# Hash-masked attention with a PReLU MLP: bits and turned q and k in one round, the last stores on ScalarE's queue, fewer products of zeros

## The chip, the cores and the metric

The kernel runs on one core of a Trainium2 chip. The metric is the device time of a whole execution in microseconds; the median of several executions is compared. A core has TensorE (PE in the profile, with PEld for its weight loads), VectorE (DVE), ScalarE (ACT), GpSimd (POOL) and SyncE (SP), which here issues most of the DMAs.

## The reference

The inputs are q, k and v of shape (4, 8, 768, 64), a projection of (64, 6), MLP weights of (512, 2048) and (2048, 512), and 2048 slopes alpha, all float32. Cut to what matters:

```python
q_bits = (einsum('bhsd,dk->bhsk', q, proj) > 0)        # the same for k
q_bucket = sum(q_bits * 2 ** arange(6))                # the same for k
mask = q_bucket[..., :, None] == k_bucket[..., None, :]
scores = where(mask, q @ k.T / sqrt(64), -1e9)
attn = exp(scores - max(scores)); attn = attn / (sum(attn) + 1e-9)
x = (attn @ v) -> (4 * 768, 512)
h = x @ w_in
out = (max(h, 0) + alpha * min(h, 0)) @ w_out
```

Each query sees only the keys whose six projected signs are the same as its own.

## The kernel before

`fast_path` does everything; a `general_path` follows that is skipped unless a flag, worked out from the sizes of the inputs, asks for it.

**Attention.** Two heads of one batch are a pair; there are 16 pairs, `pi` from 0 to 15. A pair's 768 queries are done in two halves of 384. One half of one pair is a unit, or round, `u = 2 * pi + g`, with `g` 0 or 1: 32 rounds. All instructions that go through `do(...)` keep their written order on their engine, so the loop over `u` is the order by hand; the DMA issues are placed around it. For one round the work is:

- `scores`: for each of six chunks of 128 keys, TensorE multiplies the signs of the hash bits (`qb`, `kb`, bf16) and then the turned k and q (`kT`, `qT`, f32) into one of three double banks of PSUM (tag `sc`); ScalarE writes the exponential to a tile `pt` (L706). Different bits push a score so far down that the exponential is zero. The second half of the keys of round `u` and the first half of round `u + 1` are done in one go.
- `add_first`, `add_last`, `add_total`: VectorE (L715, L720, L721, L724) and one accumulating DMA on GpSimd's queue (L716) add the six chunks to `accd`.
- `attend` and `totals`: TensorE multiplies v with the probabilities (`av`, L734) and ones with `accd` (`sm`, L746). `av` and `sm` have one buffer each.
- `divide`: VectorE takes the reciprocals of the totals, multiplies (L762) and the result `x` is stored to DRAM. The next round's `av` needs this to be done.
- `weight_abs`, `weight_parts`, `weight_sum`, `weight_sums`: one piece of the MLP weights per round is rounded and combined on ScalarE and VectorE, and stored to DRAM as the operands of a Strassen-like scheme of seven products.

Each pair needs three preparations. `turn(pi, name)` transposes q or k on TensorE (L649) and copies the result from PSUM to `qT` or `kT` (L654 on ScalarE, L652 on VectorE); these tiles have two buffers. `hash_bits(pi)` multiplies them with the projection on TensorE (L674) and writes the signs as `qb` and `kb`, seven activations on ScalarE (L682, L687). `magnitude(pi, name)` squares q or k in place on ScalarE (L660) and keeps the sums for the flag; after it the tile is free, and q or k of a later pair is loaded into it (three buffers, `qn` and `kn`). Before, rounds with `g == 0` do `hash_bits(pi + 1)`, and rounds with `g == 1` do `turn(pi + 2)` and `magnitude(pi)`, and then load pair `pi + 3`.

**The start.** `setup` fills constants and issues eight matmuls of zeros (`nil`, L512) while q and k of pair 0 are loaded in two halves, q on SyncE's queue and k on ScalarE's. Then both first halves are turned, the bits of the first half are made, and both second halves are turned. The first three chunks of scores follow.

**MLP.** From round 31 on, 8 blocks of the first layer (`f_0` to `f_7`) and 7 of the second (`z_1`, `z_2`, `z_5`, `z_6`, `z_3`, `z_7`, `z_4`) per batch run on TensorE, each itself split into seven products. A block's last step (`before.step(4)`) comes after the first step of the next. Result blocks that are complete wait in a list `to_turn`. `turn_out` transposes them on VectorE in 32 x 32 pieces (L946) and issues twelve stores of 32 KB on SyncE (L952). Only the last block, `z_4`, goes through `turn_last`: TensorE transposes it (L965), ScalarE copies it (L967), and SyncE stores it in two DMAs (L969). The tiles `o` that both use have two buffers.

Of the kernel before, what the change touches and what calls it, by code (L numbers as in the profile page):

```python
# [8 lines left out]
F32 = mybir.dt.float32  # L9
BF16 = mybir.dt.bfloat16  # L10
U32 = mybir.dt.uint32
AF = mybir.ActivationFunctionType
ALU = mybir.AluOpType
# [393 lines left out]
def fast_path(  # L407
# [12 lines left out]
    nc = tc.nc  # L420
# [37 lines left out]
    ones = const.tile([P, D], F32, name="ones")  # L458
    wh = const.tile([P, 32], F32, name="wh")
    hb = const.tile([P, 1], F32, name="hb")  # L460
    alpha16 = const.tile([NF, P], F32, name="alpha16")
    alpha = const.tile([P, NF], F32, name="alpha")
    mags = const.tile([P, 2, NPAIR], F32, name="mags")
# [27 lines left out]
    def load_part(pi, name, cs, queue):  # L491
# [4 lines left out]
        for s in range(2):  # L496
            queue.dma_start(nat[name, pi][:, cs, s], src[b, 2 * hp + s].rearrange("(p c) d -> p c d", c=NC)[:, cs])

    def setup():

        zero = const.tile([P, 512], BF16, name="zero")
        do(DVE.memset(zero, 0.0))
        do(DVE.memset(wh, 0.0))
        for s in range(2):
            nc.sync.dma_start(wh[D * s : D * s + D, :NB], proj)
        nc.sync.dma_start(alpha16, moe_alpha.rearrange("(t p) -> t p", p=P))
        make_identity(nc, ident)
        do(DVE.memset(ones, 1.0))

        ps = psum.tile([P, 512], F32, name="nil", tag="av")  # L510
        for i in range(8):
            do(PE.matmul(ps, zero[:, :P], zero, start=True, stop=True))  # L512

        do(DVE.memset(hb, 0.0))
        for r in range(0, P, 32):
            do(DVE.memset(hb[r : r + 2 * NB], 1.0 if r % D else -1.0))
            do(DVE.memset(hb[r : r + NB], -1e-37))
        for t in pts:
            do(POOL.memset(t[:, :, CW : CW + 1], 1.0))
        for t in qbs:  # L520
            do(POOL.memset(t, 0.0))
# [115 lines left out]
    def two_banks(name):  # L637
        return psum.tile([P, 2, 512], F32, name=name, tag="sc", bufs=3)
# [3 lines left out]
    def turn(pi, name, halves=BOTH, engine=None):  # L642

        src = nat[name, pi].rearrange("p c h d -> p c (h d)")
        if halves.start == 0:
            tr[name, pi] = pool.tile([P, S], F32, name=f"{name}T{pi}", tag=f"{name}T")
        ps = two_banks(f"tp_{name}{pi}")
        for c in range(CH * halves.start, CH * halves.stop):
            do(PE.transpose(ps[:, c // CH, c % CH * P :][:, :P], src[:, c], ident))  # L649
        dst = tr[name, pi].rearrange("p (h w) -> p h w", h=2)[:, halves]  # L650
        if engine is DVE:
            do(DVE.tensor_copy(dst, ps[:, halves, :CW]))  # L652
        else:
            do(ACT.activation(dst, ps[:, halves, :CW], AF.Copy, scale=DOWN if name == "q" else 1.0))  # L654
# [4 lines left out]
        n = "qk".index(name)  # L659
        do(ACT.activation(t, t, AF.Square, accum_out=mags[:, n, pi : pi + 1]))  # L660

    def hash_bits(pi, halves=BOTH):

        if halves.start == 0:
            bits["q", pi] = qbs[pi % 2]
            bits["k", pi] = pool.tile([P, S], BF16, name=f"kb{pi}", tag="kb")
        ps = two_banks(f"hs{pi}")
        for half in range(halves.start, halves.stop):  # L670
            for n, name in enumerate("kq"):
                for s in range(2):
                    r, c = D * s, D * (s ^ half) + 32 * n
                    do(PE.matmul(  # L674
                        ps[c : c + 32, half, :CW], wh[r : r + D], tr[name, pi][r : r + D, half * CW : (half + 1) * CW],
                        start=True, stop=True,
                    ))
        for half in range(halves.start, halves.stop):
            cols = slice(half * CW, (half + 1) * CW)
            for s in range(2):  # L680
                c = D * (s ^ half) + 32
                do(ACT.activation(  # L682
                    bits["q", pi][D * s : D * s + 32, cols], ps[c : c + 32, half, :CW], AF.Sign, bias=hb[c : c + 32],
                ))

            for to, c, n in [(0, 0, P)] if half == 0 else [(0, D, D), (D, 0, D)]:
                do(ACT.activation(  # L687
                    bits["k", pi][to : to + n, cols], ps[c : c + n, half, :CW], AF.Sign, bias=hb[c : c + n],
                ))


    def scores(u, half):
# [261 lines left out]
                        src[32 * a : 32 * a + 32, c],  # L954
                    )

    def turn_last():

        ((b, p, half, ch),) = to_turn
        ps = two_banks("to").rearrange("p a f -> p (a f)").rearrange("p (t i f) -> p t i f", i=2, f=P)  # L960
        o = late[0].tile([P, CH, P, 2], F32, name="o_last", tag="o")
        for ts in ((2,), (0, 1)):
            for i in range(2):
                for t in ts:
                    do(PE.transpose(ps[:, t, i], m2[b, p][:, i, t * P : (t + 1) * P], ident))  # L965
            ts = slice(ts[0], ts[-1] + 1)
            do(ACT.copy(o[:, ts].rearrange("p t f i -> p t i f"), ps[:, ts]))  # L967
            dst = out_v[b, ch * CH : (ch + 1) * CH].rearrange("c p d -> p c d")
            nc.sync.dma_start(dst[:, ts, half * 2 * P : (half + 1) * 2 * P], o[:, ts].rearrange("p t f i -> p t (f i)"))  # L969


    top = const.tile([P, 4], F32, name="top")
# [32 lines left out]
    for half in (first, second):  # L1005
        turn(0, "q", half)
        turn(0, "k", half, DVE)
        if half is first:
            hash_bits(0, first)
    load(1, "q")  # L1010
    load(1, "k")
    load_weight(0)
# [16 lines left out]
    for u in range(UNITS):  # L1029
        pi, g = divmod(u, NCH)  # L1030
        scores(u, 1)
        if u < last:
            scores(u + 1, 0)
        add_last(u)
        add_total(u)
        if u < last:
            add_first(u + 1)
        else:
            now = ff1(0, 0)
            now.step(1)  # L1040
            now.step(5)
        if g == 0 and pi + 1 < NPAIR:
            hash_bits(pi + 1)
        if g == 1 and pi + 2 < NPAIR:
            turn(pi + 2, "q")
            turn(pi + 2, "k")
        if u < last:
            weight_parts(u + 1)
        else:
            weight_sums(4)  # L1050
        attend(u, range(NC - 1))
        totals(u)
        if u < last:
            weight_sum(u + 1)
            weight_sums(1 if u < HW - 1 else 2)
            weight_group(u + 1)
        attend(u, range(NC - 1, NC))
        divide(u)
        if g == 1 and pi + 2 < NPAIR:
            load(pi + 2, "v")  # L1060
        load_weight(u + 4)
        if u == HW + 2:
            load_w(0)
            load_w(1)
            load_x(0)
        if HW + 4 <= u < HW + 8:
            sum_x(0, u - HW - 4, DVE)
        if u + 2 < NW:
            weight_abs(u + 2)
        if u == 1:  # L1070
            setup_alpha()
        if g == 1:
            for name in "qk":
                magnitude(pi, name)
                if pi + 3 < NPAIR:
                    load(pi + 3, name)


    late = []
# [5 lines left out]
    for j, (b, what, n) in enumerate(blocks):  # L1085
        n2 = n + 1 if what == "2" else 0 if n == NI - 1 else 7
        if n2 == 0:
            sides_g(b, 0)
            sum_w2(b, 0, 3, 4)
        now.step(2) if j else now.step(6)  # L1090
        if j == 0:
            now.step(3)
            now.step(7)
            now.step(2)
        now.step(22)
        if j == 4:
            largest()
        if 0 < n2 < 7:
            sides_g(b, n2)
            sum_w2(b, n2, 3, 4)  # L1100
        if n2 < 7:
            sum_g2(b, n2, 3, 4)
        if j:
            now.step(5)
            now.step(6)
            now.step(3)
            sum_w2(b, n2, 6)
            now.step(7)
            sum_w2(b, n2, 5)
            sum_g2(b, n2, 5)  # L1110
        if j == 4:
            verdict()
        if what == "1":
            load_w(b * NI + n + 2)
            if n >= NI - 2:
                load_w2(b, n - NI + 2)
        else:
            load_w2(b, n + 2)
            if b + 1 < B:
                if n == 0:  # L1120
                    load_x(b + 1)
                if n == 6:
                    for m in range(4):
                        sum_x(b + 1, m, DVE)
        turn_out()
        before = now
        if j + 1 < len(blocks):
            b1, what1, n1 = blocks[j + 1]
            now = ff1(b1, n1) if what1 == "1" else ff2(b1, n1)
            now.step(1)  # L1130
        before.step(4)
        if n2 < 7:
            sum_g2(b, n2, 6)
    turn_last()
# [1 line left out]
_INS = ['q', 'k', 'v', 'proj', 'moe_w_in', 'moe_w_out', 'moe_alpha']  # L1136
_OUTS = [((3072, 512), 'float32')]
# [25 lines left out]
```

## Time and profile before

| what | value |
|---|---|
| time, median of 4 runs | 922.04 us (920.7 to 923.46) |
| profiled execution, its own time | 923.68 us |
| its span, first to last instruction | 921.9 us |
| TensorE busy | 900.3 us (98%) |
| VectorE busy | 768.7 us (83%) |
| ScalarE busy | 409.9 us (44%) |
| GpSimd busy | 40.9 us (4%) |
| HBM traffic | 139 GB/s over the span |

The span is that of one profiled execution and runs from its first to its last instruction; the 1.8 us between span and time lie around it. All durations below come from this one execution. In rows of the timeline the first two numbers are the start and the duration in us, then come the engine, the line, the operation, its output and inputs with their shapes, and how many instructions the row holds; a bracket holds the idle time before it and what ended it. In rows by stage the columns are the stage and its length, busy time and instructions of PE, PEld, DVE, ACT and POOL, the granted clock of TensorE, the DMA share and GB/s. PEld overlaps PE. Matmuls are pipelined and their ends are modelled, so PE busy is not PE at its peak.

### The profile page before, as it was taken

The page shows a single profiled execution, that of the slowest core. Times are in us where ns is not written, and L with a number is a line of the kernel's source. Part 1 is how long each engine was busy: PE and PEld are TensorE (multiplying, and loading weights), DVE is VectorE, ACT ScalarE, POOL GpSimd, SP SyncE. Part 2 cuts the span into 40 slices and gives each one's busy share as a digit, 9 for nine tenths or more (in the row PEclk, how much of TensorE's full clock was granted, in tenths as well). Part 3 has the DMA queues.
Part 4 walks back from the last instruction along what each step waited for, and adds up shares of the span by engine and source line. Part 5 has one row for each costly group of instructions (what it writes and reads, how often), then busy time and mean ns, then how long its engine had stood idle before and what let it go on. Part 6 is the DMA issues. An engine that isn't in the chain of part 4 may idle for free.

```text
span 921.9 us, 13660 instructions
## 1 busy us (share of the span) xinstructions
PE 900.3 (98%) x4979; PEld 598.4 (65%) x4979; DVE 768.7 (83%) x1348; ACT 409.9 (44%) x735; POOL 40.9 (4%) x50
## 2 busy tenths in 40 slices
PE   8999999999999999999999999999999999999993
PEld 4444444445444444556998556998557997557993
DVE  3999998999999998677899768988768989668893
ACT  5888888888887783222112222112222112222111
POOL 1111111111111110000000000000000000000000
PEclk9999999999999999999999999999999999999997
DMA  8576979699777754435343525243525343530332
GB/s 223 148 185 171 250 179 304 163 253 251 205 189 189 190 148 126 173 117 158 123 122 106 180 91 187 93 154 79 184 84 185 103 144 87 176 120 1 140 107 55
DMA packets 133997, 141.52 MB, mean 154 GB/s; under 512 B 79760, under 2 KB 122144, under 8 KB 130336
## 3 DMA queue, kind: packets, MB, share of 16 engines
q1 hardware_dynamic: 123616, 127.57, 44.9%
q0 software_dynamic: 8704, 12.58, 8.0%
q8 instruction: 41, 0.67, 0.3%
q10 hardware_dynamic: 1600, 0.39, 0.2%
q14 instruction: 36, 0.29, 0.1%
HBM read 100.67 MB, written 27.26 MB: 139 GB/s over the span
## 4 chain that ended last, share of the span: by engine, by line
PE 59%; DVE 20%; DMA 3%; issue 1%; SPq 1%; ACT 0%; DVEq 0%; ACTq 0%
PE z_6a L808 2%; PE f_2a L808 2%; PE z_3a L808 2%; PE z_5a L808 2%; PE z_2a L808 2%; PE z_1a L808 2%; PE f_5a L808 2%; PE f_7a L808 2%; PE f_6a L808 2%; PE f_4a L808 2%; PE f_3a L808 2%; PE f_0a L808 2%; PE f_1a L808 2%; DVE accd L724 2%; PE z_7a L808 2%; DVE accd L721 2%
## 5 line engine op out<-in xcount | busy, mean ns | idle before, releaser
L706 ACT ACTIVATE pt<-sc 128x768 f32<-128x768 f32 x192 | 153.1, 814 | 62.0 <-PE sc L701 60.2
L701 PE MATMUL sc<-qT,kT 64*128 64x384 f32 x768 | 156.6, 486 | 0.0
L734 PE MATMUL av<-pt,vn 128*64 128x385 f32 (+1 forms) x768 | 136.5, 491 | 2.4 <-DVE x L762 2.4
L734 PEld LDWEIGHTS av<-pt,vn 128*64 128x64 f32 x768 | 52.3, 136 | 73.4 <-issue 61.7
L701 PEld LDWEIGHTS sc<-qT,kT 64*128 64x128 f32 x768 | 69.0, 190 | 35.0 <-issue 34.9
L858 DVE TENSOR_TENSOR g<-g,g 128x384 f32<-128x384 f32 x128 | 68.4, 555 | 2.2
L701 PE MATMUL sc<-qb,kb 64*128 64x384 bf16 x384 | 63.6, 327 | 2.4 <-ACT kb L687 1.0
L906 DVE TENSOR_TENSOR gs<-g,gs 128x768 f32<-128x768 f32 x56 | 53.4, 953 | 1.0
L898 DVE TENSOR_TENSOR ws<-wl 128x512 f32<-128x512 f32 x56 | 38.5, 688 | 18.1 <-DMA wl<-w_out_s 18.0
L906 DVE TENSOR_TENSOR gs<-g 128x768 f32<-128x768 f32 x56 | 53.4, 953 | 0.0
L716 POOL DMA_DIRECT2D accp<-pt x32 | 38.5, 1204 | 312.7 <-DVE accp L715 217.3
L701 PEld LDWEIGHTS <-kb 64*128 64x128 bf16 x384 | 19.5, 94 | 43.6 <-issue 20.9
L854 DVE SCALAR_TENSOR_TENSOR g<-h,alpha 128x384 f32<-128x384 f32 x32 | 19.8, 618 | 33.6 <-ACT h L847 33.6
L682 ACT ACTIVATE qb<-hs,hb 32x384 bf16<-32x384 f32 x64 | 36.7, 574 | 3.5 <-PE hs L674 2.4
L715 DVE TENSOR_TENSOR accp<-pt,pt 128x768 f32<-128x768 f32 x32 | 30.5, 952 | 4.4 <-ACT pt L706 4.4
L724 DVE TENSOR_TENSOR accd<-accd,accp 128x768 f32<-128x768 f32 x32 | 30.7, 958 | 3.4 <-DMA accp<-pt 2.4
L720 DVE TENSOR_TENSOR accd<-pt,pt 128x768 f32<-128x768 f32 x32 | 30.5, 953 | 3.6 <-ACT pt L706 3.5
L721 DVE TENSOR_TENSOR accd<-accd,pt 128x768 f32<-128x768 f32 x32 | 30.7, 959 | 3.3
L918 DVE TENSOR_TENSOR m<-m,m 128x768 f32<-128x768 f32 (+1 forms) x40 | 28.4, 710 | 1.0 <-ACT m L924 0.3
L687 ACT ACTIVATE kb<-hs,hb 64x384 bf16<-64x384 f32 (+1 forms) x48 | 27.7, 578 | 0.6
L746 PE MATMUL sm<-accd,ones 128*64 128x384 f32 x128 | 26.2, 488 | 0.3 <-DVE accd L724 0.3
L566 DVE TENSOR_SCALAR_CACHE_REDUCE wx<-wx 128x512 f32<-128x512 f32 x32 | 21.7, 679 | 3.1 <-ACT wx L560 3.1
(325 smaller groups left out, 1763.2 us busy)
## 6 DMA issues: line engine op xcount, KB each, us to landing
wi<-w_in_s SPq DMA_DIRECT2D x32, 896.0 KB, 4.6
wl<-w_out_s SPq DMA_DIRECT2D x28, 1024.0 KB, 4.9
accp<-pt POOLq DMA_DIRECT2D x32, 384.0 KB, 4.3
raw<-in_moe_w_in_dram SPq DMA_DIRECT2D x16, 512.0 KB, 3.9
raw<-in_moe_w_out_dram SPq DMA_DIRECT2D x16, 512.0 KB, 3.7
w_in_s<-wsi SPq DMA_DIRECT2D x16, 448.0 KB, 5.3
w_out_s<-wso SPq DMA_DIRECT2D x8, 896.0 KB, 5.4
vn<-in_v_dram SPq DMA_DIRECT2D x16, 384.0 KB, 5.5
```

The source lines that it names most:

```text
L682: do(ACT.activation(bits["q", pi][D * s : D * s + 32, cols], ps[c : c + 32, half, :CW], AF.Sign, bias=hb[c : c + 32],))
L701: do(PE.matmul(sc[:, s, :CW], what["k", pi][r, ks], what["q", pi][r, qs], start=first, stop=not first,))
L706: do(ACT.activation(pt[:, :, :CW], sc[:, :, :CW], AF.Exp, scale=SCALE / DOWN))
L715: do(DVE.tensor_tensor(accp[u], p(u, 0), p(u, 1), op=ALU.add))
L716: nc.gpsimd.dma_start(accp[u], p(u, 2), accum_op=ALU.add)
L721: do(DVE.tensor_tensor(accd[u], accd[u], p(u, 5), op=ALU.add))
L724: do(DVE.tensor_tensor(accd[u], accd[u], accp[u], op=ALU.add))
L734: do(PE.matmul(av[u][D * s : D * s + D, :w], nat["v", pi][:, s, kc * D : (kc + 1) * D], prob[u, kc][:, s, :w], start=(kc == 0), stop=(kc = ...
L808: do(PE.matmul(self.ps[bank], self.left(left, k), self.right(right, k), start=start and k == 0, stop=k == self.nk - 1, skip_group_check=no ...
L858: do(DVE.tensor_tensor(new_g(b, to)[:, i], g_m[b, x][:, i], g_m[b, y][:, i], op=ALU.subtract))
L898: do(DVE.tensor_tensor(t, w2[b, n, x], w2[b, n, y], op=op))
L906: do(DVE.tensor_tensor(t, g2[b, n, x], g2[b, n, y], op=ALU.subtract))
```

## The change

- `turn(pi + 2)` moves from rounds with `g == 1` to rounds with `g == 0`, behind `hash_bits(pi + 1)`. `qT` and `kT` have three buffers instead of two.
- `magnitude` stays in rounds with `g == 1`, but is done for pair `pi + 2`, and pair `pi + 5` is loaded after it. Pair 0 is squared in round 0, pairs 1 and 2 in round 1.
- At the start six matmuls of zeros are issued in `setup` instead of eight, and a seventh after the first halves are turned, ahead of the first half's bits.
- The first half's `kb` is made on VectorE, as a comparison and a subtraction (values of half the size), from new constants `hb_k`.
- At the end block 7 of the last batch goes through `turn_last(0)`, with one store on SyncE, in place of `turn_out`. The last block goes through `turn_last(1)`, with its two stores on ScalarE's queue.

```diff
+    hb_k = const.tile([P, 2], F32, name="hb_k")
...
-        for i in range(8):
-            do(PE.matmul(ps, zero[:, :P], zero, start=True, stop=True))
+        nil.append(lambda: do(PE.matmul(ps, zero[:, :P], zero, start=True, stop=True)))
+        for i in range(6):
+            nil[0]()
...
+        do(DVE.tensor_scalar(hb_k[:, 0:1], hb, -1.0, None, op0=ALU.mult))
+        do(DVE.memset(hb_k[:, 1:2], 0.0))
+        for r in range(0, P, 32):
+            do(DVE.memset(hb_k[r : r + 2 * NB, 1:2], 0.5))
...
-            tr[name, pi] = pool.tile([P, S], F32, name=f"{name}T{pi}", tag=f"{name}T")
+            tr[name, pi] = pool.tile([P, S], F32, name=f"{name}T{pi}", tag=f"{name}T", bufs=3)
...
-                do(ACT.activation(
-                    bits["k", pi][to : to + n, cols], ps[c : c + n, half, :CW], AF.Sign, bias=hb[c : c + n],
-                ))
+                dst, src = bits["k", pi][to : to + n, cols], ps[c : c + n, half, :CW]
+                if engine is DVE:
+                    do(DVE.tensor_scalar(
+                        dst, src, hb_k[c : c + n, 0:1], hb_k[c : c + n, 1:2], op0=ALU.is_gt, op1=ALU.subtract,
+                    ))
+                else:
+                    do(ACT.activation(dst, src, AF.Sign, bias=hb[c : c + n]))
...
-    def turn_last():
+    def turn_last(n):
-        ((b, p, half, ch),) = to_turn
+        b, p, half, ch = to_turn.pop(0)
...
-        for ts in ((2,), (0, 1)):
+        for ts in ((2,), (0, 1)) if n else ((0, 1, 2),):
...
-            nc.sync.dma_start(dst[:, ts, half * 2 * P : (half + 1) * 2 * P], o[:, ts].rearrange("p t f i -> p t (f i)"))
+            (nc.scalar if n else nc.sync).dma_start(
+                dst[:, ts, half * 2 * P : (half + 1) * 2 * P], o[:, ts].rearrange("p t f i -> p t (f i)"),
+            )
...
-            hash_bits(0, first)
+            nil[0]()
+            hash_bits(0, first, DVE)
...
-        if g == 1 and pi + 2 < NPAIR:
+        if g == 0 and pi + 2 < NPAIR:
             turn(pi + 2, "q")
             turn(pi + 2, "k")
...
-        if g == 1:
-            for name in "qk":
-                magnitude(pi, name)
-                if pi + 3 < NPAIR:
-                    load(pi + 3, name)
+        for pj in [0] if u == 0 else [] if g == 0 else [1, 2] if pi == 0 else [pi + 2]:
+            if pj < NPAIR:
+                for name in "qk":
+                    magnitude(pj, name)
+                    if pj + 3 < NPAIR:
+                        load(pj + 3, name)
...
-        turn_out()
+        if j + 1 < len(blocks):
+            turn_out()
+        else:
+            turn_last(0)
...
-    turn_last()
+    turn_last(1)
```

## The prediction

> **What bounds the kernel now.** I read the page's busy shares first, then the busy time by stage, and only then the three places where TensorE is not full: the start, the second half of the attention, the end.
>
> ```profile
> PE 900.3 (98%) x4979; PEld 598.4 (65%) x4979; DVE 768.7 (83%) x1348; ACT 409.9 (44%) x735; POOL 40.9 (4%) x50
> ```
>
> TensorE is busy for 900.3 of 921.9 us, so a change that adds no TensorE work can win only from the other 21.6 us, or from matmuls that run slower than they could. The stages (us of span, then busy us of PE, PEld, DVE, ACT, POOL) show where these lie:
>
> ```profile
> 125.00:190.00 65.00, 65.00 (x474) 31.91 (x472) 58.68 (x104) 54.33 (x83) 6.80 (x6) 1.00 0.89 236
> 250.00:310.00 60.00, 59.26 (x430) 28.71 (x432) 57.24 (x101) 48.97 (x76) 6.00 (x5) 1.00 0.75 196
> 310.00:365.00 55.00, 53.00 (x348) 25.22 (x345) 52.28 (x100) 35.85 (x55) 6.01 (x5) 1.00 0.53 139
> 909.00:922.00 13.00, 0.33 (x4) 0.09 (x1) 0.00 (x0) 0.61 (x1) 0.00 (x0) 0.61 0.27 62
> ```
>
> The middle of the attention has no gap at all on TensorE; its second half loses 2.7 us; the last 13 us are nearly empty. The end in order of time:
>
> ```profile
> 901.29 13.30 SPq L952 DMA_DIRECT2D out_dram<-o  x24
> 908.24 0.38 ACT L967 COPY o_last<-to 128x256 f32<-128x256 f32 x1 [0.70 <-DMA out_dram<-o]
> 909.37 0.61 ACT L967 COPY o_last<-to 128x512 f32<-128x512 f32 x1 [0.75 <-PE to L965]
> 914.68 1.87 SPq L969 DMA_DIRECT2D out_dram<-o_last  x2
> ```
>
> SyncE issues 24 small stores one after the other, twelve for result block 3 and twelve for block 7. The last block's tile is complete at 909.98 (909.37 + 0.61), but its two stores stand behind them and are issued from 914.68 to 916.55. The start:
>
> ```profile
> 1.19 3.59 PE L512 MATMUL nil<-zero 128*128 128x512 bf16 x8 [1.19 <-DVE wh L503]
> 5.22 0.84 PE L649 MATMUL tp_k<-ident,kn 128*128 128x128 f32 x3
> 6.72 0.85 PE L674 MATMUL hs<-kT,wh 64*32 64x384 f32 x2 [0.65 <-DVE kT L652]
> 10.44 0.50 PE L701 MATMUL sc<-qb,kb 64*128 64x384 bf16 x2 [0.74 <-DVE kT L652]
> 10.71 1.51 PE L701 MATMUL sc<-qT,kT 64*128 64x384 f32 x4
> 13.91 0.89 PE L701 MATMUL sc<-qT,kT 64*128 64x384 f32 x4
> ```
>
> Four score products take 1.51 us at 10.71 and 0.89 at 13.91 (0.81 in all later rounds): TensorE runs at half speed until about 14.2 us, although the row of granted clock says 1.00. And the rounds of the attention:
>
> ```profile
> 56.32 0.87 PE L649 MATMUL tp_q<-ident,qn 128*128 128x128 f32 x6
> 57.78 3.45 PE L734 MATMUL av<-pt,vn 128*64 128x384 f32 x20
> 129.73 0.96 DVE L720 TENSOR_TENSOR accd<-pt,pt 128x768 f32<-128x768 f32 x1 [0.59 <-ACT pt L706]
> 155.62 0.96 DVE L724 TENSOR_TENSOR accd<-accd,accp 128x768 f32<-128x768 f32 x1 [2.36 <-DMA accp<-pt]
> 214.13 4.85 ACT L706 ACTIVATE pt<-sc 128x768 f32<-128x768 f32 x6 [2.57 <-PE sc L701]
> 224.56 4.85 ACT L706 ACTIVATE pt<-sc 128x768 f32<-128x768 f32 x6 [0.73 <-PE sc L701]
> 337.79 2.48 PE L734 MATMUL av<-pt,vn 128*64 128x384 f32 x14 [0.56 <-DVE x L762]
> ```
>
> The brackets hold the idle time before an instruction. ScalarE waits 0.73 us for TensorE after a first (even) round and 2.57 after a second (odd) one. VectorE waits 0.59 once per pair of rounds until 155.62, where one accumulating transfer comes 2.36 us late; from then until the last `x` at 365.72 no VectorE row has a wait. So VectorE, not TensorE, sets the end of the attention.
>
> **The change part by part.**
>
> *Last stores.* Removed: two VectorE transposes (906.26, 1.04 us) and twelve of the 24 issues. Added for block 7: six TensorE transposes, one ScalarE copy, one 384 KB store on SyncE. Moved: the last block's two stores, to ScalarE's queue. The transposes cost 0.7 us (twelve take 1.46 in a round, 56.32 to 57.78). They go ahead of the last eight products, which waited anyway from 905.14 to 905.61 for a ScalarE copy: 0.2 us late. The copy of block 7 (0.61 for 512 columns, so about 0.85 for 768) lies between 906.1 and 907.0, before ScalarE is wanted at 907.2 to 907.4. The last block's first copy still waits for block 3's twelve stores, which use the same buffer, to land: 908.24 as before. New is that ScalarE must issue the first store between its two copies. Its four issues at the start of the kernel took 2.39 us, 0.6 each: 908.66 to 909.26, done before the second copy can start at 909.37. SyncE's own first issue took 1.4 us; at that price the second copy is 0.7 late. Second issue then at 909.98 + 0.2 = 910.2 instead of 916.16: 6.0 us earlier, 5.3 at the dearer price. The store landed 2.2 us after its issue, 918.4, and 3.5 us follow with nothing on the engines; both stay. Block 7's store is issued at about 907 and lands some 3 us later, ahead of the other. I take -5.8.
>
> Here a rule of the Trainium skill speaks against the change. "DMA: Bandwidth & Descriptors", section "Issuing engines are not separate DMA queues", says that all queues end on the same 16 engines, and that another issuing engine saves only the issue time, usually small beside the transfer. By that the gain were the 1.87 us of the two issues at most. The rows decide here: twelve issues of 0.55 us each are 6.6 us against a landing of 2.2, and they fall away as instructions; it is no bandwidth that is won. I keep the row.
>
> *Start.* Two of eight zero products go (3.59 / 8 = 0.45 each, 0.43 from start to start): the first transposes begin at 3.72 instead of 4.58, if q's first half is there. Its two loads are issued at 0.74 to 1.71 and land 2.4 to 2.5 us after issue, so by about 3.7: just there. One of them returns ahead of the hash products, in the 0.65 us in which TensorE waited for the kT copy. kb's activation (0.58) moves to VectorE (0.57 by the kT copy, same shape), which is idle then; the scores waited for the kT copy (10.29), not for kb (10.10), so this part alone is worth nothing. The new constants are six short VectorE writes (0.06 each) at 2.2 us, where VectorE idles. By the rows at unchanged speed: -0.86.
>
> The second rule: "TensorE: Matmul & The Clock Gate", section on the HAM clock gate, has the array at half clock until one free-running window of about 3.4 us was busy. Read against the trace, the doubling falls at 14.2; windows that end at 3.96, 7.38 and 10.79 each held an idle piece (before 1.19; 6.06 to 6.72; 9.69 to 10.44), the next one none. Fewer products would speak against the change, but the one that is put into the second gap leaves only 0.24 us idle, and the stretch from 1.19 to 8.9 is then longer than two windows. If it releases at 7.4: the second transposes take 0.7 instead of 1.5, scores start at 8.8, three exponentials end at 12.1 instead of 15.65, so ScalarE is 3 us earlier. Not all arrives: pair 2's k must now be turned in round 0, and its last load is issued at about 17 and lands 6.5 us later, 23.4, where TensorE at 24.79 - 3 would want it. So -1.4, not -3. I take the rule's -1.4, because the doubling in the rows has the step and the place that it describes; -0.86 stays as the other end.
>
> *Squares.* Pair 0's two squares (37.30 to 39.06, 1.76) move to round 0, where ScalarE now also has two turns (1.40, from the starts 229.33, 230.04 and 230.73) behind the bits. Before, bits end at 29.16; plus 1.40, 0.68 (weights) and 1.76 it is free at 33.0. The next round's first exponential could start at 29.46 + 1.46 (turns on TensorE) + 1.04 = 31.96. TensorE has three score buffers and stalls 0.5 us on the fourth. If ScalarE is 3 us early as above, it is free at 30.0 and there is no stall. Round 1 gets four squares (3.5), paid from its idle 2.7 plus what the turns left. Start and squares together: -1.4 warm, -0.4 cold. Eight more q and k loads come two pairs early: eight issues on SyncE at about 0.65 us, 5.3 us, ahead of a weight load that is used some 15 us later, and 1.5 MB (6 us at 250 GB/s) beside round 3's accumulating transfer (issued 47.87, lands 4.2 later, wanted at 56.2): covered by 4 us, and at worst VectorE is 2 us late where TensorE still has 3.6 in hand.
>
> *Turned q and k in the bits' round.* TensorE's rounds were 10.43 and 11.08 (totals start at 61.06, 71.49, 82.57). Transposes are 57.78 - 56.32 = 1.46, so they become 11.89 and 9.62; the sum 21.51 is unchanged. ScalarE in the long round: idle 0.73 + 1.46 - 1.40 = 0.79, still positive, no stall. The third buffer for qT and kT is why the move needs no wait. VectorE's work per round is the same, but the results of an even round come 1.46 later: in round 10 its first step on the totals started 0.49 after TensorE's last product (137.92 against 137.43), so it now waits about 1.0. With 0.59 of slack in a pair it runs 0.4 to 1.0 late when the chain without waits begins. Everything after is VectorE's own: +0.5. The odd round's products now need `x` 1.46 earlier (they had 3.6 in hand, 1.3 after 164), so TensorE stalls sooner, but since VectorE sets the end this only moves the 2.7 us of stalls.
>
> **Sum.** -5.8 - 1.4 + 0.5 = -6.7: span 915.2; the profiled execution's 923.68 would be 917.0. That execution lies 1.64 above the median of 922.04, and above all four runs. The late doubling of speed may be part of why (the window is free-running), and such a part can't be won again; I take about 1.0 of the 1.64 as staying: 916.0. A difference under 0.2% (1.8 us) can't be told from none here.
>
> **Rivals.**
> - *Clock stays late* (0.18): half speed until 14 us or longer as now, VectorE 1.0 late, dearer ScalarE issue: -0.4 + 1.0 - 5.3 = -4.7, with the same step to the median 918.2. For it: seven products are fewer than eight. Against: the filled gap.
> - *VectorE's chain falls away* (0.08): round 12's transfer is not late; the 2.7 us of TensorE stalls go: 913.3. Against: weights are still stored and loaded in that stretch (DMA share 0.89).
> - *ScalarE becomes the bound* (0.07): its long round fills 11.1 of 11.89 us. From 0.79 us more per long round TensorE waits; with 14 such rounds the change breaks even at 0.79 + 6.7 / 14 = 1.27. At 1.8 more, 14 x 1.0 - 6.7 = +7.3: 929, slower. It needs the turns and bits to cost a third more than their rows, or to start late behind transposes that lack a buffer. Against: each row's duration is steady within 2%.
> - *The stores do not do what is said* (0.07): the new queue or the tail eats all but the 1.87 us of issue: -1.4 + 0.5 - 1.0, 920.3.
>
> **How the numbers follow.** The forecast has 0.60, its own range 914.2 to 917.8. 913.0 to 919.2 takes in most of the first two rivals. Faster: 0.60 + 0.18 + 0.08 and 0.04 of the last, 0.90; same 0.05; slower 0.05.
>
> **What would show it.** End: twelve small stores instead of 24, the last two on ScalarE's queue from about 910 less the shift, 5.8 us less between the last copy and the end. Start: scores before 9.7, and 0.81 instead of 1.51 for four products there. Rounds: totals spaced 11.9 and 9.6; ScalarE's idle 0.8 and 2.5; still no VectorE wait in the second half. Wrong it is if ScalarE has no idle left in even rounds, or the last store is not issued within 1 us of the last copy.

## The result and the profile after

| | median, us | runs | ratio to before, 95% interval |
|---|---|---|---|
| before | 921.95 (920.15 to 925.27) | 55 | |
| changed | 921.0 (917.64 to 922.95) | 34 | 0.9987 [0.9981, 0.9993] |

The ratio is a gain of 1.2 us [0.6, 1.8], clear of zero but under the 0.2% that counted as a difference in the prediction. I had forecast 916.0 (913.0 to 919.2). The profiled executions differ by more, 923.68 us (span 921.9) before and 919.39 (span 917.5) after, because before's lies high and after's low among the runs. In what follows, times are told from the ratios and mechanisms from the profiles.

The changed kernel, the line of busy shares from the page, and the busy time by stage (us of span, length, then PE, PEld, DVE, ACT, POOL, granted clock, DMA share, GB/s):

```profile
PE 897.5 (98%) x4984; PEld 597.3 (65%) x4984; DVE 769.3 (84%) x1353; ACT 409.4 (45%) x735; POOL 40.9 (4%) x50
```

```profile
125.00:190.00 65.00, 64.25 (x468) 31.53 (x466) 57.99 (x104) 53.43 (x82) 7.16 (x6) 1.00 0.86 224
250.00:310.00 60.00, 58.03 (x424) 28.20 (x420) 57.14 (x105) 47.59 (x72) 6.00 (x5) 1.00 0.69 184
310.00:365.00 55.00, 52.82 (x348) 24.47 (x348) 52.41 (x96) 35.07 (x52) 6.01 (x5) 1.00 0.51 133
```

The middle of the attention, which had no gap on TensorE, now has 0.75; the second half loses 4.2 us (60 - 58.03 and 55 - 52.82) where it lost 2.7.

The end of the changed kernel, rows of SyncE's, ScalarE's and ScalarE's queue's timelines put in one order:

```profile
903.68 5.55 SPq L965 DMA_DIRECT2D out_dram<-o  x12
908.16 0.86 ACT L980 COPY o<-to 128x768 f32<-128x768 f32 x1 [0.28 <-PE to L978]
909.33 0.39 SPq L982 DMA_DIRECT2D out_dram<-o  x1
910.62 0.38 ACT L980 COPY o<-to 128x256 f32<-128x256 f32 x1 [0.76 <-DMA out_dram<-o]
911.04 0.37 ACTq L982 DMA_DIRECT2D out_dram<-o  x1
911.75 0.61 ACT L980 COPY o<-to 128x512 f32<-128x512 f32 x1 [0.75 <-PE to L978]
912.39 0.39 ACTq L982 DMA_DIRECT2D out_dram<-o  x1
```

Twelve small stores are left, and ScalarE issues each of the last two 0.03 to 0.04 us after the copy that fills it. SyncE has issued block 7's store by 909.72, ahead of both of these copies: by these rows the last two stores would have found nothing ahead of them on its queue either, now that twelve stores are gone. What ScalarE's queue adds to that, no run separates. From the end of the last copy (912.36) to the end of the span are 5.1 us; before, they were 11.9 (909.98 to 921.9). But the last copy comes 2.4 us later than before: what the end gained, something ahead of it lost. The start and the first rounds:

```profile
1.19 2.74 PE L514 MATMUL nil<-zero 128*128 128x512 bf16 x6 [1.19 <-DVE wh L506]
4.36 0.87 PE L658 MATMUL tp_q<-ident,qn 128*128 128x128 f32 x3 [0.43 <-DMA qn<-in_q_dram]
8.76 0.68 DVE L698 TENSOR_SCALAR kb<-hs,hb_k 128x384 bf16<-128x384 f32 x1 [2.28 <-ACT qb L691]
9.49 0.34 PE L714 MATMUL sc<-qb,kb 64*128 64x384 bf16 x2 [1.30 <-DVE kb L698]
24.75 0.85 PE L658 MATMUL tp_k<-ident,kn 128*128 128x128 f32 x6 [1.81 <-DMA kn<-in_k_dram]
42.99 0.34 PE L714 MATMUL sc<-qb,kb 64*128 64x384 bf16 x2 [1.22 <-DVE alpha L535]
```

TensorE has finished six zero products and waits 0.43 for q's load; the scores start at 9.49, ahead of the 9.7 that the prediction named as a sign, and wait there for VectorE's new kb; kb in turn starts at 8.76 only when ScalarE has written qb. Round 0 has a wait of 1.81 for pair 2's k, and round 2 one of 1.22 for the copy of alpha. The rounds after (start of the totals on TensorE, the exponentials on ScalarE, the late row on VectorE):

```profile
61.49 0.82 PE L759 MATMUL sm<-accd,ones 128*64 128x384 f32 x4
73.38 0.81 PE L759 MATMUL sm<-accd,ones 128*64 128x384 f32 x4
83.00 0.81 PE L759 MATMUL sm<-accd,ones 128*64 128x384 f32 x4
75.87 4.85 ACT L719 ACTIVATE pt<-sc 128x768 f32<-128x768 f32 x6 [0.82 <-PE sc L714]
85.49 4.85 ACT L719 ACTIVATE pt<-sc 128x768 f32<-128x768 f32 x6 [2.54 <-PE sc L714]
158.09 0.96 DVE L737 TENSOR_TENSOR accd<-accd,accp 128x768 f32<-128x768 f32 x1 [2.76 <-DMA accp<-pt]
```

Totals 11.89 and 9.62 apart, ScalarE idle 0.82 and 2.54: the cadence is the forecast one to 0.05. The late transfer of round 12 is still there, 2.76 after 2.36.

### The profile page after: what moved, and what is told of

The parts are those of the page before. It is cut to its first block, busy times and chain, and to the rows that moved or that the text cites. A ratio compares the mean times of both kernels' runs of the same rounds, so it can differ in the third digit from the quotient of the medians.

```text
span 917.5 us, 13669 instructions
## 1 busy us (share of the span) xinstructions
PE 897.5 (98%) x4984; PEld 597.3 (65%) x4984; DVE 769.3 (84%) x1353; ACT 409.4 (45%) x735; POOL 40.9 (4%) x50
## 4 chain that ended last, share of the span: by engine, by line
PE 65%; DVE 15%; DMA 2%; issue 1%; SPq 1%; ACT 0%; DVEq 0%; ACTq 0%
PE sc L714 3%; PE av L747 3%; PE f_2a L821 2%; PE z_3a L821 2%; PE z_2a L821 2%; PE z_6a L821 2%; PE z_5a L821 2%; PE z_1a L821 2%; PE f_6a L821 2%; PE f_4a L821 2%; PE f_1a L821 2%; PE f_5a L821 2%; PE f_3a L821 2%; PE f_7a L821 2%; PE f_0a L821 2%; PE z_7a L821 2%
```

## The experiments

"Turned rounds" below are the moved turns and squares with the third buffers, "new end" the last stores, "new start" the zero products and pair 0's kb. Where two variants are compared, the difference is that of their ratios to the kernel before, times 922, with the two half-widths added in quadrature.

### Which part does what

**e1_end**: the kernel before with the new end alone.

```diff
-        turn_out()
+        if j + 1 < len(blocks):
+            turn_out()
+        else:
+            turn_last(0)
...
-    turn_last()
+    turn_last(1)
```

> The kernel before with the new end alone: block 7 of the last batch through turn_last(0), the last two stores on ScalarE's queue. Theory A (the end is worth its price, and the rounds give it back): 6 us faster, ratio about 0.9935, and the stretch from the last copy's end to the end of the span falls from 11.9 to about 5.1 us. Theory B (the end itself gives little outside a profile): at most 1.9 us faster, ratio 0.998 or above.

Measured: 915.82, ratio 0.9941 [0.9928, 0.9954], a gain of 5.4 us [4.2, 6.6].

**e2_start**: the kernel before with the new start alone.

```diff
-        for i in range(8):
-            do(PE.matmul(ps, zero[:, :P], zero, start=True, stop=True))
+        nil.append(lambda: do(PE.matmul(ps, zero[:, :P], zero, start=True, stop=True)))
+        for i in range(6):
+            nil[0]()
...
-            hash_bits(0, first)
+            nil[0]()
+            hash_bits(0, first, DVE)
```

> The kernel before with the new start alone: six products of zeros and a seventh ahead of the first bits, first kb on VectorE. Theory A (the start helps): TensorE at full speed from about 7 us, round 0's totals 2 us or more earlier than 28.07, and 1.4 to 3 us faster, ratio 0.9967 to 0.9985. Theory B (what the start gains is lost again because VectorE's chain sets the end of the attention): totals of round 0 earlier, but the last x of the attention no earlier than 365; ratio 0.999 to 1.001.

Measured: 925.29, ratio 1.0034 [1.0016, 1.0052], a loss of 3.1 us [1.5, 4.8].

**e3_rounds**: the kernel before with the turned rounds alone.

```diff
-            tr[name, pi] = pool.tile([P, S], F32, name=f"{name}T{pi}", tag=f"{name}T")
+            tr[name, pi] = pool.tile([P, S], F32, name=f"{name}T{pi}", tag=f"{name}T", bufs=3)
...
-        if g == 1 and pi + 2 < NPAIR:
+        if g == 0 and pi + 2 < NPAIR:
             turn(pi + 2, "q")
             turn(pi + 2, "k")
...
-        if g == 1:
-            for name in "qk":
-                magnitude(pi, name)
-                if pi + 3 < NPAIR:
-                    load(pi + 3, name)
+        for pj in [0] if u == 0 else [] if g == 0 else [1, 2] if pi == 0 else [pi + 2]:
...
```

> The kernel before with the moved turns and squares alone (bits and turns in one round, third buffer for qT and kT). Theory A (uneven rounds give back the gain): slower by 4 to 6 us, ratio 1.0045 to 1.0065: 1.2 us at round 2's third score product, which waits for the copy of alpha, and 2 to 2.5 us because VectorE's chain without waits begins later, and a wait for pair 2's k. Theory B (the rounds cost what was forecast, 0.5 to 1 us): ratio 1.0005 to 1.001.

Measured: 925.2, ratio 1.0041 [1.0028, 1.0054], a loss of 3.8 us [2.6, 5.0].

**e4_start_end**: the changed kernel without the turned rounds (the diffs of e1 and e2 together).

> The changed kernel without the moved turns and squares: the new start and the new end. Theory A: the sum of the two, 7 to 8.5 us faster, ratio 0.991 to 0.9925. Theory B (start without worth): as the end alone, 0.9935. If the rounds are innocent, it is no faster than the changed kernel, 0.9987.

Measured: 916.73, ratio 0.9946 [0.9933, 0.9959].

What follows: the new end brings 5.4. The turned rounds cost 3.8 on top of the kernel before (e3), and e4, which lacks them, is 3.8 +/- 1.3 faster than the changed kernel (0.9946 against 0.9987). The new start brings nothing beside the new end (0.9946 against 0.9941). With the 3.8 of e3, the sum -5.4 + 3.8 + 0.5 = -1.1 stands beside the measured -1.2.

Alone the new start lost 3.1, and why stays open. Its profile has one lead, at the old end, which e4 does not have. The last copy ends at 910.08 (909.98 in the profile of before), but SyncE's 24 issues take 14.69 us instead of 13.30:

```profile
901.38 14.69 SPq L965 DMA_DIRECT2D out_dram<-o  x24
916.17 0.87 SPq L982 DMA_DIRECT2D out_dram<-o_last  x2
```

In e3, which has the old end too, they take 14.88. One profile of each cannot show that this is the loss.

The trace of e1 bears on the clock at the start. With all eight zero products, as before the change:

```profile
1.20 3.59 PE L512 MATMUL nil<-zero 128*128 128x512 bf16 x8 [1.20 <-DVE wh L503]
6.72 0.51 PE L674 MATMUL hs<-kT,wh 64*32 64x384 f32 x2 [0.65 <-DVE kT L652]
9.49 0.34 PE L701 MATMUL sc<-qb,kb 64*128 64x384 bf16 x2 [1.12 <-ACT kb L687]
```

Its hash products take 0.51 at 6.72 (0.85 in the profile of before) and its scores start at 9.49, at the same time as in the changed kernel. The late doubling of speed is in one of the six profiles with the old start (that of before; not in e1, e3, e6, e10 and e11). Of the eight with the new start it is in one as well, e2: hash products of 0.85 at 6.62, scores at 10.23. It came with single executions, and the edit did not decide it.

### Is it VectorE's chain from round 12?

**e5_after_late** and **e6_end_late**: the changed kernel, and e1, with the first two loads of w_in held back behind a VectorE write that stands in round 18.

```diff
             w_m[n] = mid.tile([P, NM, 2, P], F32, name=f"wi{n}", tag="wi")
+            if n < 2:
+                do(DVE.memset(w_m[n][:, 0, 0, 0:2], 0.0))
             nc.sync.dma_start(w_m[n], w_in_s[n % NI])
```

> The changed kernel; the first two loads of w_in (896 KB each), which SyncE issues at 145.3 to 147.9 us of the span beside four stores of 448 KB and the accumulating transfer of round 12, are held back until round 18 (a two-element write by VectorE into each buffer comes ahead of them). Theory A (the transfer of round 12 comes late because of that traffic, VectorE's chain starts there and is never made up, so what the rounds cost is what this transfer is late): the wait of 2.76 for accp at 158.09 falls under 0.5, the last x at 368.55 comes about 2.3 us earlier, and the time falls from 921.0 to about 918.7. Theory B (the uneven rounds themselves keep VectorE late): the wait may go, VectorE stays behind from another cause, the last x moves by under 0.7 and the time stays at 920.3 to 921.3. Either way round 18 or 19 may show a late transfer of its own; then the last x moves little and this run cannot tell A from B.

> The kernel before with the new end only (915.82 in the first set), and the same two loads held back until round 18. Theory A: the wait of 2.65 for accp at 154.84 falls under 0.5 and the time falls by about 2.2, to 913.6; the distance to the changed kernel with the same hold falls from 5 to about 3 or less, since both lose the same late transfer. Theory B: the wait goes here too, but the distance to the changed kernel stays at 4 to 5 us. If no wait on VectorE was deciding, 915.5 to 916.

Measured: e5 919.84, ratio 0.997 [0.9955, 0.9985], 1.6 +/- 1.5 better than the changed kernel; e6 913.93, ratio 0.9901 [0.9882, 0.9921], better than e1 by 1.9 in the medians and 3.7 +/- 2.2 in the ratios. In both traces VectorE's wait in round 12 is gone (the next wait for a transfer is 0.22 at 242.84 and 0.61 at 239.41). So the late transfer does cost time, in either order of rounds, but the distance between the two kernels did not shrink to 3: it is 0.9970 - 0.9901, 6.4 +/- 2.3 us. Theory A falls as the explanation of what the rounds cost. The trace of e5 held the hint. Round 0:

```profile
22.50 0.85 PE L658 MATMUL tp_q<-ident,qn 128*128 128x128 f32 x6 [0.99 <-DMA qn<-in_q_dram]
24.58 1.15 PE L658 MATMUL tp_k<-ident,kn 128*128 128x128 f32 x6 [1.24 <-DMA kn<-in_k_dram]
```

Two waits for pair 2's loads, and the second turn takes 1.15 instead of 0.85: TensorE's clock has dropped (0.66 from 25 to 30 us, by stage).

### Round 0 and the first waits

**e7_after_alpha**: the changed kernel; ScalarE copies alpha.

```diff
-        do(DVE.tensor_copy(alpha, ps))
+        do(ACT.copy(alpha, ps))
```

> The changed kernel; the copy of the turned alpha out of its score buffer is made by ScalarE at the end of round 1, not by VectorE. The wait of 1.22 us of TensorE at 42.99 (a third score product for the buffer that VectorE still holds) goes or shrinks to 0.3, and the totals of round 2 start at 50.7 and not 51.87. Theory A (VectorE's chain from round 12 on sets the end of the attention, early losses of TensorE are made up before): the time stays within 0.5 of 921.0. Theory C (what TensorE loses in rounds 0 to 2 is handed on to the end): 919.8.

Measured: 920.81, ratio 0.9975 [0.9962, 0.9989], 1.1 +/- 1.4 better than the changed kernel: inconclusive. The edit only moved the stall. The copy stands ahead of round 1's four squares in ScalarE's order and waits for TensorE's transpose, so the squares and the exponentials behind them are late:

```profile
42.08 0.17 ACT L535 COPY alpha<-alps 128x16 f32<-128x16 f32 x1 [3.35 <-PE alps L534]
46.30 0.34 PE L714 MATMUL sc<-qb,kb 64*128 64x384 bf16 x2 [1.74 <-ACT pt L719]
```

**e8_after_load2**: the changed kernel; pair 2's loads are issued earlier.

```diff
     load(0, "v")
+    load(2, "q")
+    load(2, "k")
     for i in range(1, 3):
         load_weight(i)
     load(1, "v")
-    load(2, "q")
-    load(2, "k")
```

> The changed kernel; the four loads of pair 2's q and k are issued ahead of two weight loads and pair 1's v, some 4 us earlier. TensorE's wait of 1.81 us for kn at 24.75 falls under 0.3 and the totals of round 0 start at about 27.2 and not 28.81; pair 1's v and the weights of rounds 1 and 2 land some 2 us later, with room. Theory A: the time stays within 0.5 of 921.0, because VectorE's chain sets the end from round 12. Theory C (losses of rounds 0 to 2 are handed on): 919.4.

Measured: 924.55, ratio 1.0018 [1.0002, 1.0034], 2.9 +/- 1.6 slower than the changed kernel. TensorE's wait for kn is gone, and a longer one stands in its place: the weights that were pushed back are now 3.98 late on ScalarE, the exponentials behind them too, and TensorE waits 4.24.

```profile
21.07 0.66 ACT L569 ACTIVATE wx<-raw 128x512 f32<-128x512 f32 x1 [3.98 <-DMA raw<-in_moe_w_in_dram]
22.48 0.51 PE L714 MATMUL sc<-qb,kb 64*128 64x384 bf16 x2 [4.24 <-ACT pt L719]
```

The first 20 us have no spare place for pair 2's loads (DMA share 1.03 and 1.18 from 10 to 15 and 15 to 20 us in the changed kernel). Its turn, not its load, had to move.

**e9_after_turn2**: the changed kernel; pair 2 alone is turned in round 1, all later pairs as in the change.

```diff
-        if g == 0 and pi + 2 < NPAIR:
+        if g == (pi == 0) and pi + 2 < NPAIR:
             turn(pi + 2, "q")
             turn(pi + 2, "k")
```

> The changed kernel; pair 2's q and k alone are turned in round 1, as before the change, and all later pairs in the bits' round. Theory D (what the rounds cost is paid once, in round 0: TensorE waits 1.8 to 2.5 us for pair 2's late loads, in two of the six profiles with this order it then also ran at 0.63 of its clock from 24 to 28 us, and in the rounds that follow TensorE has no slack to make it up): no wait for qn or kn in round 0, clock 1.00 there, and the time falls by about 2.5, to 918.5 (at least 917.8). Theory B (the uneven rounds themselves, whose even totals come 1.46 later when VectorE's chain begins, keep the end late): 920.3 to 921.3.

Measured: 917.87, ratio 0.9946 [0.9933, 0.9959], 3.8 +/- 1.3 better than the changed kernel. That is as much as the turned rounds cost: e4, which has none of them, is at 0.9946 too. Theory D holds, and theory B falls as the explanation of the 3.8. (The expectation's "six profiles" is a slip: there are five, those of the changed kernel, e3, e5, e7 and e8.) One thing is not separated. e9 has no alpha stall (TensorE's wait for the copy of alpha) in round 2, while the changed kernel waits 1.22 there and e4 waits 1.81:

```profile
41.69 0.34 PE L714 MATMUL sc<-qb,kb 64*128 64x384 bf16 x2 [1.81 <-DVE alpha L535]
```

So e9 is rid of two waits, that for pair 2's loads and this one, and in its profile it is 1.47 us ahead of e4 in round 3 (totals at 58.73 against 60.20), while the measured times of the two are equal. The uneven rounds may cost about as much as e4's stall does; no run prices that stall cleanly (e7 moved it, and e10's gain lies inside its uncertainty).

The totals of rounds 0, 1 and 2, first in the changed kernel, then in e9:

```profile
28.81 0.81 PE L759 MATMUL sm<-accd,ones 128*64 128x384 f32 x4
38.43 0.81 PE L759 MATMUL sm<-accd,ones 128*64 128x384 f32 x4
51.87 0.81 PE L759 MATMUL sm<-accd,ones 128*64 128x384 f32 x4
```

```profile
25.31 0.81 PE L759 MATMUL sm<-accd,ones 128*64 128x384 f32 x4
36.76 0.81 PE L759 MATMUL sm<-accd,ones 128*64 128x384 f32 x4
49.11 0.81 PE L759 MATMUL sm<-accd,ones 128*64 128x384 f32 x4
```

Of the 3.50 in round 0, 1.46 is the turn that e9 does later; the other 2.04 are lost. By round 1, with the same turns done in both, the loss is 1.67. By round 2 it is 2.76; the 1.09 more come with the changed kernel's alpha stall. The last `x` of the attention starts at 365.28 in e9,

```profile
365.28 0.62 DVE L775 SCALAR_TENSOR_TENSOR x<-av,vs,dn 128x384 f32<-128x384 f32 x1
```

and at 367.93 in the changed kernel: 2.65 later. The loss of the first three rounds arrives at the end of the attention almost whole, although both traces have a late transfer in round 12 (3.34 and 2.76). It arrives because TensorE has no slack behind it: from round 2 to round 10 the totals take 86.04 us in both, which is four times the 21.51 of a pair. (Behind the attention the profile of e9 loses 3.6 us waiting for weights, in z_4, z_3 and f_2, where the changed kernel's waits for none: this execution, 921.48, is the slowest of e9's six. The gain of 3.8 is that of the six, not of this profile.)

**e12_after_fill**: the changed kernel with products of zeros in round 0's waits.

```diff
+        nil.append(zero)
...
         ps = two_banks(f"tp_{name}{pi}")
+        for i in range({"q": 4, "k": 3}[name] if pi == 2 else 0):
+            do(PE.matmul(ps[:, 0], nil[1][:, :P], nil[1], start=True, stop=True))
         for c in range(CH * halves.start, CH * halves.stop):
```

> The changed kernel; in round 0 seven more products of zeros (four ahead of the turn of pair 2's q, three ahead of k's, into the buffer that the turn then overwrites) stand where TensorE waits for the loads. The loads land no earlier. If the half clock of some executions after that wait is part of the cost: clock 1.00 from 24 to 28 us and 0.5 to 1.0 us faster than the changed kernel, about 920.2. If the wait alone counts: 920.7 to 921.3, or a few tenths more where the products outlast the wait.

Measured: 919.45, ratio 0.9966 [0.9953, 0.9979], 1.9 +/- 1.3 better than the changed kernel, with loads that land no earlier. So the dropped clock is a real part of the cost; the interval, 0.6 to 3.2, takes in the 0.5 to 1.0 that I expected. Stage 24 to 28 us, first e7 and then e12 (the clock is the third figure from the end of a line):

```profile
24.00:28.00 4.00, 3.27 (x16) 1.91 (x16) 3.83 (x8) 3.92 (x7) 1.20 (x1) 0.63 0.56 154
```

```profile
24.00:28.00 4.00, 3.96 (x27) 2.12 (x26) 3.86 (x8) 3.94 (x8) 1.20 (x1) 1.00 0.17 37
```

Its price by the rows: from the start of k's turn to the totals of round 0 e7 needs 30.80 - 25.16 = 5.64, the changed kernel's profile, at full clock, 28.81 - 24.75 = 4.06. That is 1.6 us in an execution that it befalls. With the 2.76 of the undisturbed pair of profiles, and the clock low in some executions, the 3.8 comes out: 2.76 + 1.6 x 0.65, where the share of 0.65 is fitted, not counted. The mean granted clock of each execution gives a rough count: of 36 recorded executions of the changed kernel (two more than in the table) 21 have 0.998 or 0.999 and take 920.3 on average, 15 have 0.995 to 0.997 and take 921.6. Four us at 0.63 lower the mean by 0.37 x 4 / 917.5 = 0.0016. With a share of 15 in 36 the sum is 3.4, inside 3.8 +/- 1.3. It is rough because e1, which has none of these waits, has 0.996 or 0.997 in three of its six.

### A version that beats both, and one that shows what the squares are for

**e10_best**: e6, with alpha copied by ScalarE behind the squares.

```diff
-        do(DVE.tensor_copy(alpha, ps))
+        do(ACT.copy(alpha, ps))
...
-        if u == 1:
-            setup_alpha()
         if g == 1:
             for name in "qk":
                 magnitude(pi, name)
                 if pi + 3 < NPAIR:
                     load(pi + 3, name)
+        if u == 1:
+            setup_alpha()
```

> The kernel before with the new end and the two loads of w_in held back (913.93 in the last set), and now the copy of the turned alpha made by ScalarE behind round 1's two squares. TensorE's wait of 2.26 us at 42.04 for that buffer falls under 0.5. If TensorE's early losses are handed on (theory C): about 912.6, since VectorE's chain takes over from about round 20 and gives part back. If not: 913.5 to 914.2.

Measured: 913.31, ratio 0.9899 [0.9884, 0.9914], 9.3 us faster than before and the fastest of all. The alpha stall is gone (totals of round 2 at 46.87, in e6 49.47). Against e6 the gain of 0.6 in the medians is inside the uncertainty. In its trace the 2.6 that TensorE won early shrank to 0.9 by the end of the last `x` (363.32 against 364.25), with another late transfer on the way:

```profile
238.48 0.96 DVE L724 TENSOR_TENSOR accd<-accd,accp 128x768 f32<-128x768 f32 x1 [2.28 <-DMA accp<-pt]
```

**e11_best_turns**: e10 with the moved turns (pair 2's in round 1), third buffers, and squares where they were before.

```diff
-            tr[name, pi] = pool.tile([P, S], F32, name=f"{name}T{pi}", tag=f"{name}T")
+            tr[name, pi] = pool.tile([P, S], F32, name=f"{name}T{pi}", tag=f"{name}T", bufs=3)
...
-        if g == 1 and pi + 2 < NPAIR:
+        if g == (pi == 0) and pi + 2 < NPAIR:
```

> The kernel of the run before this one (e10), with q and k of pairs 3 to 15 turned in the bits' round (third buffers for qT and kT), pair 2's in round 1 and the squares where they were: the uneven rounds alone, without the early loads. Theory D: within 0.8 of that kernel. Theory B: 2 to 4 us slower than it.

Measured: 948.69, ratio 1.0276 [1.0246, 1.0306], 35 us slower than e10. Both theories missed it, and the reason is my edit, not the uneven rounds. The loads of pair pi + 3 stand behind the squares of pair pi, which I had left in the odd round; the turn one round later then meets its load late in every pair. TensorE's waits for kn, three of thirteen:

```profile
73.72 0.85 PE L649 MATMUL tp_k<-ident,kn 128*128 128x128 f32 x6 [1.96 <-DMA kn<-in_k_dram]
97.30 1.44 PE L649 MATMUL tp_k<-ident,kn 128*128 128x128 f32 x6 [1.87 <-DMA kn<-in_k_dram]
123.46 0.85 PE L649 MATMUL tp_k<-ident,kn 128*128 128x128 f32 x6 [2.83 <-DMA kn<-in_k_dram]
```

It is the changed kernel's round 0, thirteen times over: a wait of 1.65 to 3.08 us, and in four of the thirteen a turn at near half speed behind it (1.34 to 1.51 instead of 0.85). It also shows that the moved squares are no ornament of the change: they bring the loads forward by as much as the turn needs. Round 0 is the one place where they can't.

## Why the prediction was wrong, point by point

The step that failed is the wait for pair 2's loads in round 0. The prediction saw it, about 1.6 us, and set it against a gain of 3 us at the start that the edit does not bring. So the turned rounds stood at +0.5 and cost 3.8, and the start stood at -1.4 and brought nothing that shows beside the new end. The largest term, the end, was right.

- **Last stores, -5.8.** Right: 5.4 [4.2, 6.6]. Twelve issues are gone, and nothing queues behind the rest. ScalarE's issue cost 0.37 to 0.39 where I allowed 0.6 to 1.4, and the second copy was never behind the first issue. That ScalarE's queue was needed for it is not shown, since SyncE was free from 909.72. The Trainium skill's "DMA: Bandwidth & Descriptors", section "Issuing engines are not separate DMA queues", says that another issuing engine saves only issue time, and that does not speak against the result: I had booked 1.87 us for it, but the issue time ahead of the last stores was the 13.30 us of 24 stores.
- **Start, -1.4.** Wrong: +0.5 +/- 1.7 with the new end, a loss alone. Two steps failed. "I take the rule's -1.4, because the doubling in the rows has the step and the place that it describes": what the rule of the Trainium skill's "TensorE: Matmul & The Clock Gate", part 1, explained was one execution. Its own remark that the window is free-running said that the next execution may differ, and e1 and e3 do: at the old start they have fast hash products at 6.72. What one profile seems to promise from the clock's phase was no property of the edit. And the -0.86 by the rows failed as well: q's load let TensorE start at 4.36, 0.22 earlier and not 0.86, and the scores then waited for kb, which VectorE begins only when ScalarE has written qb. At full clock the scores start between 9.15 and 9.49 with the old start (five profiles) and between 8.83 and 9.58 with the new one (seven).
- **Turned rounds, +0.5.** Mis-sized: +3.8. The cadence, ScalarE's idle times and the sum of 21.51 are as forecast, and e9, which keeps them, is as fast as e4; to +/- 1.7 they cost no more than e4's alpha stall does. What failed stands in the step on the start: "pair 2's k must now be turned in round 0, and its last load is issued at about 17 and lands 6.5 us later, 23.4, where TensorE at 24.79 - 3 would want it". I saw the wait and let it eat a gain (-3 down to -1.4). That gain did not exist, since TensorE is as early in five of the six profiles with the old start (e1, e3, e6, e10, e11); so the same wait was a loss of 2.04 in round 0, and I had booked none.
- **"So VectorE, not TensorE, sets the end of the attention", and early losses are absorbed.** Wrong for losses. I read that VectorE has no wait after 155.62 and took what happens to TensorE before as covered. But where TensorE is full for eight rounds, its delay is carried to where VectorE's chain begins, and the chain starts as much later: 2.76 at round 2 was 2.65 at the last `x`. In these profiles a gain ahead of the chain was partly lost there (e10 against e6), and this loss was not.
- **The alpha stall.** Not in the prediction at all. In the profile of before, TensorE does not wait for VectorE's copy. In e1, e4 and e6, where the first totals come 2.6 to 2.7 us earlier, it waits 1.70, 1.81 and 2.26, and in the changed kernel 1.22. e2, 1.96 us earlier than before, has no such wait.
- **The median.** I let 1.0 of the 1.64 between before's profile and its median stay. Taken from the median itself, my -6.7 would have given 915.3, so this step did not make the miss. With the measured parts, -5.4 + 0.5 + 3.8 from the median gives 920.9 against 921.0.
- **Rivals.** "ScalarE becomes the bound" did not happen (0.82 idle in long rounds), nor did the stores fail. "Clock stays late" had the right suspect in the wrong place: the clock falls in round 0, behind the new waits. A wait for pair 2's loads belonged among the rivals, with its price of 2 to 4 us. Three of the rivals' totals do not follow from their terms: "clock stays late" comes to 918.0 and not 918.2, "ScalarE becomes the bound" to 930 and not 929, and "the stores do not do what is said", with the 1.87 that its words leave, to 919.9 and not 920.3.
- **The signs.** Nearly all that I had listed as proof came true, scores at 9.49, totals 11.89 and 9.62 apart, idle 0.82 and 2.54, twelve stores (the stretch behind the last copy fell by 6.8 and not 5.8), and the sum was still wrong by five. None of them looked at the first totals of round 0, the only place where a moved turn meets a load that was not moved.

## What to carry to other kernels

When a step is moved ahead of where it was, look at its first instance: steady rounds have their loads early, the first one has the start's full queues ahead of it, and here that one wait was paid to the end, because the engine behind it was full. Don't book a gain from a clock phase that a single profile shows; an execution of another variant with the same start tells whether it is the kernel's. And list a sign for each term of the sum at the place where that term could fail, not where it is sure to hold.

## What the runs showed of the hardware

TensorE's clock dropped after waits that were short. The section on the oscillation of the HAM clock gate in the Trainium skill's "TensorE: Matmul & The Clock Gate" warns of idle gaps over some 3.4 us. Here two gaps of 1.26 and 0.73 us within 3 us were followed by a granted clock of 0.63 from 24 to 28 us (e7; in stages of 1 us it is 0.50 from 26 to 28), and two of 0.99 and 1.24 by 0.62 (e5). One of 4.24 was followed by 0.50 from 23 to 25 us (e8). One of 1.81 (the changed kernel) and two of 1.18 and 0.88 (e3) were not, and in e11 four of thirteen waits of 1.65 to 3.08 had a slow turn behind them. What decides is not shown. It is a price that some executions pay; in the one profile with products of zeros in the gaps the clock stayed at 1.00.

ScalarE's queue takes a store of 128 to 256 KB in 0.37 to 0.39 us. SyncE's twelve small stores take 5.55 together, 0.46 each, and the 24 of the kernel before 13.30 (14.69 in e2, 14.88 in e3). Both kernels store the same bytes there; what differs is the number of stores.
